# 768 unreachable matmuls and fifteen small loads in a gated decode kernel (attention beside a SwiGLU block)

## The chip, the core and the metric

The kernel runs on one core of one Trainium2 chip. Its time is the device time of one launch, in microseconds (us). The core has five engines, each with its own instruction stream: TensorE (PE in the profile; its weight loads are listed as PEld), VectorE (DVE), ScalarE (ACT), GpSimd (POOL) and SyncE (SP). Data is moved between the chip's memory (HBM) and the on-chip memory by 16 DMA engines, which take their work from queues. The engines wait for each other through semaphores; a DMA adds 16 to its semaphore in all, in steps as its shares land.

## The reference

One token `x` of 512 numbers goes through two blocks, and a gate mixes their results:

```python
def _A_ref(x, k_cache, v_cache, wq, wo):        # 32 query heads, 8 key/value heads, 32768 cached keys of 128
    q = (x @ wq) ...                            # by heads
    scores = einsum("bhqd,bhkd->bhqk", q, repeat(k_cache, 4)) * (128 ** -0.5)
    p = softmax(scores)
    o = einsum("bhqk,bhkd->bhqd", p, repeat(v_cache, 4))
    return o.reshape(1, 1, 4096) @ wo

def _B_ref(x, w_gate, w_up, w_down):            # 512 -> 1792 -> 512
    return (silu(x @ w_gate) * (x @ w_up)) @ w_down

g = sigmoid((x * gate_w).sum(-1))
return g * _A_ref(x, ...) + (1 - g) * _B_ref(x, ...)
```

All tensors are bf16. `k_cache` and `v_cache` are 64 MB each in powers of two (8 x 32768 x 128 x 2 bytes); they and the weights are read once, and the result is one row of 512 numbers.

## The kernel before

**Tiling.** The cache of one key/value head (a "group" of 4 query heads) is 8 MB of K and 8 MB of V. On chip the kernel keeps five pages of 32 KB a partition (`page`, line 177). Partition p holds the cached rows 256p to 256p + 255; each half of a group (128 rows a partition) fills one page. `load_k` and `load_v` are the functions on SyncE's queue that load a whole group of K or V, mostly with one DMA of 8 MB.

**Stages.** TensorE first computes q from `wq` and the two projections of the second block (`emit_start`). Then a loop of eight passes, one a group, does for K: transposes of 128x128 (`emit_fill`, line 371) into `pst`, copied to `ktT` by VectorE (line 765), then the scores (`emit_scores`, line 383) into `ps_sc`. The maximum is taken, ScalarE computes the exponentials into `ET`, and in the next pass TensorE multiplies them with V (`emit_v`, line 440) and reduces the sums (`emit_reduce`). When the loop is done, `emit_end` handles the last V, the product with `w_down` (`wd`, and a last part of it in `wz`), and begins the product with `wo`.

**The order on SyncE's queue.** It is written out by hand: `wq`, `w_gate`, `w_up`, K of group 0; then for g = 1 to 7 K of group g and V of group g - 1; then the last V, `wd` (line 350), two loads of the remaining 128 rows of `w_down` (line 358), and `wo` in five pieces (line 363). Most loads wait, on SyncE, until TensorE has done with the page that they overwrite: `load_k` on `sem_fill` (line 311), `load_v` on `sem_v_free` (line 335).

**TensorE's program.** It is written in another order than it runs. A loop of two turns holds two conditional parts: `emit_end`, for the second turn, stands first; `emit_start`, with the loop of eight passes in it, stands behind it and is taken in the first turn. Behind this whole block stands a tail that all engines have: TensorE adds the remaining pieces of `wo` (`emit_wo`, line 246, each piece behind a wait for its load), VectorE copies the sum into `res_row` (line 818), and SyncE and ScalarE each store half of it (line 270); SyncE then waits for both stores (line 822). Counted in the code, TensorE's program has 824 matmuls, each with a weight load of its own, and some 55 other instructions: about 1,700. Of these the loop of eight passes has about 1,080.

`emit_strip` is the helper that does one matmul of one column of weights against 512 columns. `PAD = 768` is already there: a tile `pad` of 768 bytes a partition, that nobody writes or reads.

## Time and profile before

| | |
|---|---|
| time, median of two runs | 349.05 us (348.97 to 349.12) |
| profiled execution: its time | 349.16 us |
| its span, first to last instruction | 347.8 us |
| bytes read from HBM | 148.11 MB, 426 GB/s over the span |
| busy: PE, PEld, DVE, ACT, POOL | 260.8, 220.6, 186.6, 33.4, 4.6 us |
| granted TensorE clock, mean | 0.851 |

The span is what the profile lists, from the first instruction of the program to the last; 1.4 us of the profiled execution's time lie around it. "Busy" is the time in which an engine worked; an engine's idle time is listed with what ended it. The chain of work is followed back from the last instruction, at each step to what released it, so its shares say what set the end. A DMA queue's share is the time that its packets took, out of the time of all 16 DMA engines. SPq stands for SyncE as an issuer of DMAs. "x" and a number is a count.

### The profile page before, as it was taken

To read this page: it belongs to the slowest core of one execution; us is meant where nothing else is said; L and a number is where in the kernel's file an instruction comes from. 1 tells how busy PE (TensorE), PEld (TensorE's weight loads), DVE (VectorE), ACT (ScalarE), POOL (GpSimd) and SP (SyncE) were. 2 spreads that over 40 slices of the span, in tenths; PEclk is the share of its full clock that TensorE was granted. 3 is DMA by queue.
4 is the path that set the end of the run, shared out by engine and by line. 5 is a ranking of instruction groups with operands and counts; after the bars stand their busy time and mean duration, and the time that the engine had idled before them with its cause. 6 is when DMAs were issued, how large, how long until landed. Compare 5 with 4: busy or idle time off the path is not lost.

```text
span 347.8 us, 8869 instructions
## 1 busy us (share of the span) xinstructions
PE 260.8 (75%) x3925; PEld 220.6 (63%) x3925; DVE 186.6 (54%) x232; ACT 33.4 (10%) x143; POOL 4.6 (1%) x16
## 2 busy tenths in 40 slices
PE   1354995999749982999459982999469972999475
PEld 1124994998449941997259942996269842996232
DVE  3144995698119931697129921895149820895101
ACT  1002000300130003000300003000400012000400
POOL 3000000000000000000000000000000000002000
PEclk9996999699659987699959985898869985898669
DMA  8999999999999999999999999999999999999996
GB/s 322 419 459 426 420 422 458 469 414 437 414 430 475 415 437 415 437 467 415 437 407 445 467 414 437 407 452 460 414 437 407 452 460 415 437 407 452 406 418 261
DMA packets 3946, 148.21 MB, mean 426 GB/s; under 512 B 450, under 2 KB 580, under 8 KB 868
## 3 DMA queue, kind: packets, MB, share of 16 engines
q1 hardware_dynamic: 3932, 148.11, 98.7%
q8 instruction: 6, 0.10, 0.1%
q10 hardware_dynamic: 8, 0.00, 0.0%
HBM read 148.11 MB, written 0.00 MB: 426 GB/s over the span
## 4 chain that ended last, share of the span: by engine, by line
DMA 64%; PE 33%; DVE 2%; issue 1%; SPq 1%; ACT 0%; DVEq 0%
DMA page<-in_A_k_cache_dram 52%; PE pst L371 24%; DMA page<-in_B_w_up_dram 6%; DMA page<-in_A_wo_dram 6%; PE ps_sc L383 5%; PE ps_o L440 2%; PE pst L535 1%; DVE ktT L722 1%; DVE ktT L765 0%; SPq L363 0%; PE ps_m L553 0%; PE ps_m L566 0%; DVE ktT L712 0%; DVE ktT L710 0%; PE ps_sc L246 0%
## 5 line engine op out<-in xcount | busy, mean ns | idle before, releaser
L765 DVE COPY ktT<-pst 128x2048 bf16<-128x2048 bf16 x128 | 153.3, 1221 | 64.6 <-PE pst L371 60.4
L371 PE MATMUL pst<-ident_f,page 128*128 128x128 f32 x1024 | 147.2, 299 | 39.5 <-DMA page<-in_A_k_cache_dram 38.2
L371 PEld LDWEIGHTS pst<-ident_f,page 128*128 128x128 f32 x1024 | 126.0, 154 | 43.9 <-DMA page<-in_A_k_cache_dram 38.8
L383 PE MATMUL ps_sc<-qcur,ktT 128*128 128x8 bf16 x2048 | 64.1, 166 | 6.3 <-DVE ktT L765 6.3
L383 PEld LDWEIGHTS ps_sc<-qcur,ktT 128*128 128x128 bf16 x2048 | 63.8, 97 | 8.0 <-DVE ktT L765 7.1
L440 PE MATMUL ps_o<-page,ET 128*16 128x512 bf16 x512 | 39.4, 477 | 5.5 <-DMA page<-in_A_v_cache_dram 5.5
L440 PEld LDWEIGHTS ps_o<-page,ET 128*16 128x16 bf16 x512 | 15.0, 107 | 26.1 <-issue 18.8
L633 ACT ACTIVATE ET<-ps_sc,nbias 128x128 bf16 x64 | 23.9, 555 | 49.9 <-DVE nbias L791 49.9
L626 ACT ACTIVATE acc<-ps_o 128x512 f32<-128x512 f32 x8 | 4.8, 597 | 223.8 <-PE ps_o L440 218.9
L783 DVE TENSOR_REDUCE gm<-ps_m 4x1 f32<-4x128 f32 x8 | 2.2, 279 | 40.6 <-PE ps_m L420 40.6
L633 ACT ACTIVATION_READ_ACCUMULATOR ET<-ps_sc,nbias 128x1 f32 x64 | 18.3, 285 | 0.0
L773 DVE TENSOR_REDUCE pmaxf<-ps_sc 128x4 f32<-128x512 f32 x16 | 11.0, 686 | 8.4 <-PE ps_sc L383 8.4
L497 PE MATMUL pst<-page,xT 128*1 128x512 bf16 x32 | 3.6, 627 | 8.9 <-DMA page<-in_A_wq_dram 8.9
L461 PE MATMUL ps_m<-sel,acc 128*128 128x4 f32 x64 | 8.4, 255 | 1.8 <-ACT acc L626 1.6
L461 PEld LDWEIGHTS ps_m<-sel,acc 128*128 128x128 f32 x64 | 7.7, 191 | 2.5 <-ACT acc L626 2.2
L424 PE MATMUL ps_m<-diag,ones_f 4*128 4x4 f32 x16 | 3.8, 306 | 6.8 <-DVE diag L787 6.8
L424 PEld LDWEIGHTS ps_m<-diag,ones_f 4*128 4x128 f32 x16 | 3.3, 259 | 8.4 <-issue 8.4
L750 DVE RECIPROCAL rS<-ps_m 128x4 f32<-128x4 f32 x9 | 1.6, 182 | 12.2 <-PE ps_m L461 12.2
L497 PEld LDWEIGHTS pst<-page,xT 128*1 128x1 bf16 x32 | 0.9, 115 | 10.7 <-issue 10.7
L685 DVE CAST ktT<-pst 128x1024 bf16<-128x1024 f32 x2 | 2.4, 1220 | 8.2 <-PE pst L497 8.2
L452 PEld LDWEIGHTS ps_m<-esum,ones_f 128*128 128x128 f32 x32 | 4.2, 190 | 3.5 <-issue 3.5
L301 POOL MEMSET page<- 48x2048 bf16 x1 | 1.8, 1798 | 311.7 <-PE pst L371 311.7
(76 smaller groups left out, 54.6 us busy)
## 6 DMA issues: line engine op xcount, KB each, us to landing
page<-in_A_k_cache_dram SPq DMA_DIRECT2D x4, 4096.0 KB, 34.9
page<-in_A_wq_dram SPq DMA_DIRECT2D x1, 4096.0 KB, 13.4
page<-in_A_wo_dram SPq DMA_DIRECT2D x1, 2048.0 KB, 17.4
page<-in_B_w_gate_dram SPq DMA_DIRECT2D x1, 1792.0 KB, 17.2
page<-in_B_w_up_dram SPq DMA_DIRECT2D x1, 1792.0 KB, 21.0
wd<-in_B_w_down_dram SPq DMA_DIRECT2D x1, 1664.0 KB, 30.3
page<-in_A_wo_dram SPq DMA_DIRECT2D x1, 1152.0 KB, 19.8
page<-in_A_wo_dram SPq DMA_DIRECT2D x1, 512.0 KB, 20.6
```

The source lines that it names most:

```text
L371: ins = pe.transpose(pst[u % NST][:, k * 128 : (k + 1) * 128], kv[:, n * 128 : (n + 1) * 128], ident_f[:, :],)
L383: ins = pe.matmul(ps_sc[b][:, col : col + 2 * HPG], kt[:, k, e, :], qcur[:, e, :], start=(e == 0), stop=(e == 1),)
L424: pe.matmul(ps_m[:, M_B0 : M_B0 + HPG], ones_f[0:HPG, :], diag[:, :], start=True, stop=True,).then_inc(sem_b, STEP)
L440: ins = pe.matmul(ps_o[32 * c : 32 * c + RQ * HPG, :], ET[:, n : n + RQ, :].rearrange("p n h -> p (n h)"), v[:, k * RQ : (k + 1) * RQ, :], ...
L452: pe.matmul(ps_m[:, M_S0 : M_S0 + HPG], ones_f[:, :], esum[:, b, :], start=(b == 0), stop=(b == NB - 1),)
L461: ins = pe.matmul(ps_m[:, M_P0 : M_P0 + HPG], acc[:, q, :], sel4[:, q * HPG : (q + 1) * HPG], start=(q == 0), stop=(q == RQ - 1),)
L497: ins = pe.matmul(pst[0][32 * k : 32 * k + 1, t * QN : (t + 1) * QN], xT[:, c : c + 1], wq_v[:, c, n : n + QN], start=(c == 0), stop=(c == ...
L535: ins = pe.matmul(pst[1][32 * k : 32 * k + 1, w * 512 : w * 512 + FS], xT[:, c : c + 1], wgu[:, w, c, k * FS : (k + 1) * FS], start=(c == ...
L626: act.activation(part, ps_o[:, :], ACT.Copy).then_inc(sem_acc, STEP)
L633: act.activation(ET[:, b * R : (b + 1) * R, h], sc[:, h, bass.ds(bank, R)], ACT.Exp, bias=nbias[:, h : h + 1], scale=SCALE, accum_out=esum ...
L765: dve.tensor_copy(ktT[:, n % NKT, :], pst[n % NST][:, :].bitcast(BF16)).then_inc(sem_cp, 1)
L773: dve.tensor_reduce(pmaxf[:, b, :], sc, AX.X, ALU.max).then_inc(sem_d, 1)
```

## The change

There are two additions; nothing is removed.

Behind the last matmul of TensorE's program stands a loop of two turns with two nested conditions, `turn > 0` and `turn < 1`. They exclude each other, so the 768 calls of `emit_strip` inside never run. TensorE runs the loop's own register instructions and branches, and skips the body.

On SyncE's queue there are fifteen new loads. The first takes 15 rows of 64 numbers (128 bytes each) from `A_wq` into the new tile `mark`, the next 14, and so on down to 1. One is issued behind each `load_k` and each `load_v` of the loop over the groups, and one behind the last `load_v`. Nobody reads `mark`. At the end SyncE waits for the fifteen loads, ahead of its wait for the stores.

```diff
+    MARKS = list(range(15, 0, -1))
+    PAD = 768
...
+        sem_mark = S_("s_mark")
...
         res_row = T("res_row", [128, 128], BF16)
+        mark = T("mark", [16, len(MARKS), 64], BF16)
...
+                marks = list(enumerate(MARKS))
+
+                def load_mark():
+                    if marks:
+                        m, n = marks.pop(0)
+                        sp.dma_start(mark[0:n, m, :], A_wq[0:n, 0:64]).then_inc(sem_mark, 16)
+
...
                 load_k(0)
                 for g in range(1, G):
                     load_k(g)
+                    load_mark()
                     load_v(g - 1)
+                    load_mark()
                 load_v(G - 1)
+                load_mark()
+                assert not marks
...
         for k in range(1, len(sem_wo)):
             ins = emit_wo(pe, k)
         ins.then_inc(sem_pe_sum, 1)
+        with pe.Fori(0, 2, 1) as turn:
+            with pe.If(turn > 0):
+                with pe.If(turn < 1):
+                    for _ in range(PAD):
+                        emit_strip(pe, wd, tT, 0, True, True)
         act.wait_ge(sem_pe_part, 1)
...
             emit_store(eng, half, res_row)
+        sp.wait_ge(sem_mark, 16 * len(MARKS))
         sp.wait_ge(sem_out, 32)
```

## The prediction

> **What bounds the kernel now.** I read the page's DMA part first, because the kernel reads everything once.

> ```profile
> q1 hardware_dynamic: 3932, 148.11, 98.7%
> q8 instruction: 6, 0.10, 0.1%
> q10 hardware_dynamic: 8, 0.00, 0.0%
> HBM read 148.11 MB, written 0.00 MB: 426 GB/s over the span
> ```

> SyncE's queue (q1) alone keeps the 16 DMA engines occupied for 98.7% of 347.8 us, or 343.3 us. Its first packet starts at 1.8 us and the last piece of `wo` lands at 345.9 us. So there is no hole in the stream: the time is the bytes over the rate, and what comes ahead and behind. The second row matters for this change: six packets of 16 KB (0.10 MB) that are instructions. The chain of waits, cut to its end, shows the tail:

> ```profile
> 324.78 20.75 DMA page<-in_A_wo_dram
> 345.53 0.04 issue
> 345.57 0.29 PE ps_sc L246 x8
> 345.87 0.04 issue
> 345.90 0.27 PE ps_sc L246 x4
> 346.17 0.02 issue
> 346.19 0.29 DVE res_row L818
> ```

> `wo` is issued at 323.5 to 325.3 us, is served 20 us later behind what was queued, and once it lands only 0.6 us of work and the store are left. The last of SyncE's instructions, the wait for the store, is at 347.82 us.

> When do the instruction packets run? The DMA view of 66 to 348 us answers:

> ```profile
> DMA packets 2881, 120.39 MB, mean 427 GB/s; under 512 B 336, under 2 KB 464, under 8 KB 752
> ...
> q1 hardware_dynamic: 2877, 120.39, 98.7%
> q10 hardware_dynamic: 4, 0.00, 0.0%
> ```

> There is no q8 row. The six packets start at 5.0, 36.8, 44.9, 51.3, 57.1 and 64.5 us. TensorE walks its loop of eight passes for the first time from 33 to 61 us; no other engine has a program that long. So I take them for TensorE's program, fetched block by block as it first gets there. Seven further passes, the jump back to `emit_end` and the tail fetch nothing: all of it stays on chip.

> **One fetch is felt by one DMA engine.** The steps in which a load's semaphore rises show its 16 shares. The first page of K, after one fetch, has 15 shares by 31.30 us and one at 32.29; V of group 0, after six, has ten shares from 79.02 to 79.66 and six from 80.58 to 80.98. So each fetch put another engine about 1.2 us behind, and it stays behind. The two small loads of the rest of `w_down` (line 358) then occupy four of the early ten for 0.61 us each time. At the end six shares of the last `wo` piece land from 344.13 to 344.33 and ten from 345.34 to 345.86: the slowest engine sets the end, and levelling all 16 would gain at most (345.86 - 344.2) x 6/16 = 0.6 us.

> **The change, part by part.**

> *The fifteen loads: bytes.* They move 15 + 14 + ... + 1 = 120 rows of 128 bytes, 15 KB. What counts is the engine that gets a share of each. A packet of 256 bytes took 15 ns, a semaphore packet 9 ns. For what lies between loads I compare the pieces of `wo` on the early engines: landings at 341.89, 343.15, 343.79, 344.13, so 1.26, 0.64 and 0.34 us for pieces of 4, 2 and 1 KB a row. Doubling the last gives 0.68 against 0.64: the fixed part of one load is at most 0.04 us. So a small load costs an engine between 0.02 and 0.06 us, and fifteen cost between 0 (an early engine gets them) and 0.9 us (the last engine gets all). I take 0.1 us, since most engines get fewer and the first ones to be served need not be the last.

> [...]

> *The fifteen loads: SyncE.* An issue costs SyncE 0.33 to 0.78 us (lines 311 and 358). It is hidden where SyncE waits anyway:

> ```profile
> SPq L311 <- PE pst L371: 130.6, 6, 28.7
> SPq L335 <- PE ps_o L440: 103.1, 6, 17.7
> ...
> SPq L335 <- PE pst L371: 22.8, 1, 22.8
> ...
> SPq L358 <- POOL page L301: 11.3, 1, 11.3
> ```

> Each of these waits is many times one issue. Two loads have no wait ahead of them and come later by one issue: V of group 0 (issued at 44.3, landed at 81.0) and `wd` (305.7, landed at 336.0). Both stand in the queue for 30 us and more, so the cost is nothing; without that cover it would be 0.4 to 0.8 us each. The added wait at the end stands ahead of the wait for the stores; the loads it asks for landed long before, so it costs one semaphore instruction, 0.02 us.

> *The 768 matmuls.* They add 1,536 instructions to some 1,700. None runs, but TensorE has to get past them. After the last wait for `wo` (345.90 us) it dispatches four matmuls and reaches the new loop at about 346.1. On the first turn it jumps over the whole body; the target lies 1,536 instructions on. Six packets or more hold the program of 1,700, so a block has under 290 instructions, and the target is some five blocks further, in one that was never fetched: the engine must wait for it. On the second turn the same target is on chip. VectorE's copy and the stores don't wait for this; the end of TensorE's program does.

> Nothing in the trace shows a jump to an absent block, so I bound it. From below: the store, on idle queues, is issued at 346.51 and its first data have landed at 347.61, 1.1 us; a 16 KB packet takes 0.61 us; 1.7 us together. From above: the second fetch of the trace cannot have been asked for before the loop began at 33.0, and its packet ended at 37.7 (36.83 + 0.88): 4.7 us, under a full load of data. The queues are idle at the end, so I stay nearer to the lower row and take 2.4 us. TensorE is through at 346.1 + 2.4 + 0.2 for the second turn = 348.7, against 347.82 for SyncE's last wait now: +0.9 us. At the lower end it is +0.2, at the upper one +3.2; and nothing if the end of TensorE's program is not what the time waits for.

> [...]

> *Sum.* 349.16 (profiled) + 0.1 + 0.0 + 0.9 = 350.2. The median before is 0.1 lower than the profiled execution, so I say 350.0 to the nearest half.

> **The rivals.**

> 1. *The jump hides.* The fetch is under 1.7 us, or the time does not wait for TensorE's end: 349.1 to 349.3. For it: 1.7 us pass between 346.1 and 347.8 anyway. Chance 0.25. Should the dead code not be in the program at all, the time is the same.
> 2. *The loop no longer stays on chip (slower).* If TensorE's fetches run ahead into the added blocks and push out blocks of the loop, the loop (1,080 instructions at under 290 a block) fetches about five blocks on each of seven passes. [...] For it: six blocks and what was there at the start are little over the program now, so there may be no more room. Against it: the dead code is never approached before the end, and the fetches of before went one block ahead only. Chance 0.10, nearly all of it above 356.
>    [...]
> 3. *Another engine is last.* The small loads, or other places for the fetched blocks, put the 1.2 us of a fetch and the 1.2 us of line 358's loads on one engine: +1.2 on top, 350.3 to 351.5. Chance 0.08.
> 4. *The small loads level the engines.* At most 0.6 us gained: 348.5. Chance 0.05; anything faster by more than that would need fewer bytes, 0.02.

> The forecast itself keeps 0.50. Within 2% (342.1 to 356.0, about what a measurement of this kernel can tell from no change) lie the forecast and rivals 1, 3 and 4: 0.88. Slower by over 2%: 0.10; faster: 0.02. The range must hold forecast, rival 1 and rival 3: from 348.8 to 353.0, which takes in the upper bound of the fetch (349.05 + 3.2 + 0.1 = 352.4).

> **What would show it.** In the profile of the changed kernel: fifteen more loads and no later landing of K and V than before; q8 with six packets until 66 us as before, and one or two more at 346 us or later; SyncE's last wait near 347.9; a gap on TensorE's sequencer behind the last matmul. q8 packets between 66 and 340 us would make rival 2 true and the prediction wrong; so would a hole in q1's stream behind a small load.

## The result, and the profile after

| | before | after |
|---|---|---|
| time, median (two runs each) | 349.05 us | 353.05 us (352.83 to 353.27) |
| ratio to before | | 1.0111, 95% interval 1.0094 to 1.0127 |
| profiled execution: time | 349.16 us | 352.83 us |
| its span | 347.84 us | 351.24 us |
| last share of `wo` landed | 345.86 us | 346.49 us |
| SyncE's last wait ended | 347.84 us | 348.54 us |

The change costs 4.0 us, or 1.1%. The forecast was 350.0 us, 0.95 us over before, in a range of 348.8 to 353.0: the direction and the main mechanism were right, the size was a quarter of what came, and the median lies 0.05 us above the upper end of the range.

The DMA part of the page of the changed kernel (queue, packets, MB, share of 16 engines):

```profile
q1 hardware_dynamic: 4172, 148.13, 97.9%
q8 instruction: 8, 0.13, 0.1%
q10 hardware_dynamic: 8, 0.00, 0.0%
HBM read 148.13 MB, written 0.00 MB: 422 GB/s over the span
```

q1 has 240 packets more, 120 of data and 120 of semaphores, and the instruction queue has two packets more. When these run is seen in the DMA view of two stretches of the changed kernel. From 66 to 346 us there is no instruction packet:

```profile
DMA packets 3076, 120.53 MB, mean 430 GB/s; under 512 B 534, under 2 KB 657, under 8 KB 945
...
q1 hardware_dynamic: 3076, 120.53, 99.6%
```

and from 346 to 352 us there are two, which the trace puts at 347.70 to 348.64 and 350.76 to 351.84 us:

```profile
q8 instruction: 2, 0.03, 2.1%
q1 hardware_dynamic: 13, 0.01, 0.3%
```

The end of the chain of waits, which follows the data and not TensorE's sequencer, is what it was, 0.69 us later:

```profile
325.57 20.92 DMA page<-in_A_wo_dram
346.49 0.04 issue
346.53 0.33 PE ps_sc L250 x4
346.86 0.02 issue
346.88 0.29 DVE res_row L838
```

SyncE still has time for its fifteen additional issues; its waits for pages, in the view of the DMA queue's own waits, are as long as before but for 5 us in all (130.6, 103.1 and 22.8 us before):

```profile
SPq L315 <- PE pst L386: 129.3, 6, 27.8
SPq L339 <- PE ps_o L455: 100.6, 6, 17.4
...
SPq L339 <- PE pst L386: 21.2, 1, 21.2
```

What comes last now is TensorE's sequencer, the part that runs the engine's register instructions and branches (PEldq in the rows). The views of the lines of the new loop (line 830 is the loop, lines 831 and 832 its outer and inner condition) give minimum, median and maximum in ns, then the first and the last start in us:

```profile
L831 PEldq COMPARE_BRANCH  x2: 77/1694/3310, 346.7 to 350.6; - x2
```

```profile
L832 PEldq COMPARE_BRANCH  x1: 217/217/217, 350.7 to 350.7; - x1
```

```profile
L830 PEldq MOVE  x3: 29/35/38, 346.5 to 350.5; - x3
L830 PEldq ALU_OP  x2: 36/36/36, 350.1 to 351.1; - x2
L830 PEldq COMPARE_BRANCH  x2: 76/158/240, 350.2 to 351.2; - x2
```

The branch of line 831 takes 3,310 ns on the first turn, where it jumps over the body, and 77 ns on the second, where it doesn't. On the second turn the inner condition jumps over the same body, and that takes 217 ns: what costs is the first jump to this place and not the distance. The first jump starts at 346.73 and ends at 350.04; the rest of the two turns ends with the span at 351.24, 2.70 us behind SyncE's last wait. In the span the 3.40 us are therefore 0.70 (everything up to the stores is later) and 2.70 (TensorE's sequencer behind them). Another 0.27 us lie outside the span (352.83 - 351.24 = 1.59 against 1.32). Its cause is open: 1.59 us lie outside in each of the three profiled executions that end with TensorE's program (this one and those with 768 and 192 matmuls below), though the second packet ends 0.6, 1.0 and 0.5 us behind the last instruction, and 1.3 to 1.4 us in all the others.

### The profile page after: what moved, and what is told of

The parts are those of the page before. It is cut to its first block, busy times and chain, and to the rows that moved or that the text cites. A ratio compares the mean times of both kernels' runs of the same rounds, so it can differ in the third digit from the quotient of the medians.

```text
span 351.2 us, 8894 instructions
## 1 busy us (share of the span) xinstructions
PE 260.5 (74%) x3925; PEld 220.3 (63%) x3925; DVE 186.7 (53%) x232; ACT 33.4 (10%) x143; POOL 4.6 (1%) x16
## 4 chain that ended last, share of the span: by engine, by line
DMA 63%; PE 32%; DVE 2%; issue 1%; SPq 1%; ACT 0%; DVEq 0%
DMA page<-in_A_k_cache_dram 51%; PE pst L386 23%; DMA page<-in_B_w_up_dram 6%; DMA page<-in_A_wo_dram 6%; PE ps_sc L398 5%; PE ps_o L455 2%; DVE ktT L780 1%; PE pst L550 1%; DVE ktT L737 1%; SPq L378 0%; PE ps_m L568 0%; PE ps_m L581 0%; DVE ktT L727 0%; DVE ktT L725 0%; ACT ktT L634 0%
```

## The experiments

Theory A: the jump goes to a block of the program that is not on chip, and TensorE's end comes last. Theory B: the small loads cost most. Theory C: a program twice as long disturbs the loop. All times of "before" below are medians of the runs made beside the experiment: 349.23 us for the body in `emit_start` and for the loads of one, twelve and sixteen rows, 349.15 us for the others.

### Only the unreachable matmuls

```diff
         ins.then_inc(sem_pe_sum, 1)
+        with pe.Fori(0, 2, 1) as turn:
+            with pe.If(turn > 0):
+                with pe.If(turn < 1):
+                    for _ in range(768):
+                        emit_strip(pe, wd, tT, 0, True, True)
```

> Only the 768 unreachable matmuls, without the fifteen loads. Theory A (the jump over the body goes to a block that is not on chip, and TensorE's end comes last): the branch takes about 3.3 us as in the changed kernel, its last instruction is 4.5 to 4.7 us behind the landing of the last piece of wo, and the time is +3.3 us (2.7 at least, 3.6 at most) over the kernel before. Theory B (the small loads cost most, by slowing the stream): under +1 us. Theory C (a program twice as long disturbs the loop): instruction packets between 66 and 340 us and a later landing of wo; A and B expect none and a landing as before, 345.9 us.

Measured: 352.45 us, ratio 1.0093 (1.0077 to 1.0108), +3.3 us. The last share of `wo` landed at 345.89 us, 0.03 later than before, and there is no instruction packet between 66 and 346 us. The branch over the body, in the view of its line:

```profile
L816 PEldq COMPARE_BRANCH  x2: 77/1874/3670, 346.1 to 350.3; - x2
```

Its 3.67 us can be split by the packet that it waits for: it starts at 346.13, the packet at 347.14 (1.0 us later), the packet takes 1.26 us, and the branch ends at 349.80, 1.4 us behind it. The other instructions of the two turns take 1.2 us more, to 351.02, which is 5.1 us behind the landing of `wo` and not 4.5 to 4.7. So theory A holds for 3.3 of the 4.0 us; B and C don't.

### Only the fifteen loads

```diff
+                def load_mark(): ...            # as in the changed kernel
...
+        sp.wait_ge(sem_mark, 16 * len(MARKS))
```

> Only the fifteen small loads, without the unreachable matmuls. Theory A: the time is what the stream loses, +0.5 to +0.7 us (the last piece of wo landed 0.63 us later in the changed kernel), and the span ends with SyncE's wait for the stores. Theory B: +3 to +4 us. If the 0.63 us was scatter between executions and not the loads: +0.0 to +0.2 us.

Measured: 349.73 us, ratio 1.0016 (1.0007 to 1.0025), +0.6 us. All 16 shares of the last `wo` piece came 0.59 us later on average, the last at 346.40 instead of 345.86. (The rows name no engine, so shares are compared in order of landing. In the four kernels of this section that leave out the loads and have the body behind or ahead of the tail, the mean differs from before by -0.08 to +0.01 us, single shares by up to 0.33.) With the run before this accounts for the whole change: 349.15 + 3.3 + 0.6 = 353.05.

### A shorter body: 128 and 192 matmuls

```diff
-                    for _ in range(768):
+                    for _ in range(128):        # and 192 in the other kernel
```

> 128 unreachable matmuls (256 instructions) and no small loads. [...] Theory A: the branch takes 0.1 to 0.3 us, no instruction packet behind 340 us, TensorE is through before the stores have landed, and the time is within 0.2 us of before. If the cost is that of the loop and its branches whatever they jump over: as much as with 768, +3.3 us. If it goes by the length of the body: a sixth, +0.5 us.

> [...] Theory A: a step, the branch takes 3.3 us again, one instruction packet behind 345 us or two, and the time is +2.7 to +3.6 us over the kernel before, as with 768. [...]

Measured: 349.22 us with 128 (ratio 1.0001, 0.9992 to 1.0010) and 352.56 us with 192 (ratio 1.0094, 1.0078 to 1.0109). The branch over the body with 128:

```profile
L816 PEldq COMPARE_BRANCH  x2: 77/202/328, 346.1 to 347.0; - x2
```

and with 192:

```profile
L816 PEldq COMPARE_BRANCH  x2: 77/1944/3810, 346.3 to 350.6; - x2
```

### The same body where the jump is hidden

The body stands in `emit_start`, ahead of the wait for `wq`.

```diff
                     pe.wait_ge(sem_dve_x, 1)
+                    with pe.Fori(0, 2, 1) as late:
+                        with pe.If(late > 0):
+                            with pe.If(late < 1):
+                                for _ in range(768):
+                                    emit_strip(pe, wd, tT, 0, True, True)
                     pe.wait_ge(sem_q, 16)
```

> The 768 unreachable matmuls stand in the first stage, ahead of TensorE's wait for wq, and no small loads. Theory A (what costs is a jump to an absent block at a place where the end waits for it): the jump falls at about 5 us, takes 3 to 4 us, and is hidden, since wq lands at 14.1 us; there are 7 to 9 instruction packets instead of 6, none behind 345 us unless the tail crosses into a new block; a second stall of up to 4 us may come at 316 us, where emit_end's block may have been replaced, and is hidden by loads that are queued until 336 us. Time -0.1 to +0.7 us. If the program's length itself costs (theory C): +3.3 us again, with instruction packets in every pass of the loop.

Measured: 350.55 us, ratio 1.0044 (1.0030 to 1.0058), +1.3 us: more than theory A said. The jump over the body and the jump from the loop back to `emit_end` both stall, in the view of their lines:

```profile
L493 PEldq COMPARE_BRANCH  x2: 77/2948/5818, 6.6 to 13.0; - x2
```

```profile
L609 PEldq COMPARE_BRANCH  x2: 67/3724/7381, 324.0 to 343.0; - x2
```

The first ends at 12.4 us, with `wq` landed at 14.3; the second ends at 331.4, with the last V landed at 333.4. Neither delays anything, though under a full load of data they take 5.8 and 7.4 us. In the kernel before the jump back to `emit_end` takes 209 ns (its line 604) and no instruction packet runs near it; here one starts at 329.1 us, and what it brings no row shows. What costs are the packets:

```profile
q1 hardware_dynamic: 3932, 148.11, 98.3%
q8 instruction: 11, 0.18, 0.2%
```

Eleven instead of six, where seven to nine were expected. The two early additional ones put two more shares of the stream 1.0 to 1.2 us behind. Three late ones start at 329.1, 334.6 and 343.2 us, and each puts a share that is late already another 1.2 us behind: one share of the last V (333.35), two of `wd` (337.29 and 337.43), three of the last `wo` piece (347.05 to 347.19). In the kernel before the last one lands at 345.86. So an instruction packet beside the stream is not free here: it puts shares about 1.2 us behind, and as these shares were late already, the last share of `wo` moved by 1.3 us.

### The same body ahead of the tail

```diff
+        with pe.Fori(0, 2, 1) as turn: ...      # the body of 768
         pe.wait_ge(sem_part, 1)
```

> The 768 unreachable matmuls stand ahead of the tail, between the first piece of wo and TensorE's wait for ScalarE's copy, and no small loads. Theory A: the same jump, with the same 3.3 to 3.8 us and 1.2 us for the rest of its two turns, but it begins at about 341.5 us, when TensorE would wait for the copy until 343.2 and for the last piece of wo until 345.9 anyway; the tail starts at 346.0 to 346.6 and needs 1.2 us, so the stores are 0.8 to 1.5 us late and nothing of TensorE's comes behind them: time +0.8 to +1.8 us, half of what it costs at the end. A cost that goes with the length of the program would be +3.3 us here too.

This expectation failed. Of six executions two took 352.93 and 353.42 us, 3.8 and 4.3 us more than before, and four took 360.0 to 360.1; none of the four was profiled, so what took 6.6 us more there stays open. In the profiled one (353.42) the jump starts at 343.1 and not at 341.5, because TensorE first goes through a drain and the barrier that ends the block (342.0 to 342.8), which I had not counted.

```profile
L811 PEldq COMPARE_BRANCH  x2: 77/1932/3787, 343.1 to 347.4; - x2
```

The end of the chain of waits of this kernel shows the other thing that I had wrong:

```profile
343.40 4.65 issue
348.05 2.38 PE ps_sc L246 x72
350.42 0.02 issue
350.45 0.29 DVE res_row L823
```

With nothing left to wait for, the tail's 72 matmuls take 2.4 us and not 1.2. They run at a granted clock of 0.50 here (348.0 to 350.5 us), where the kernel before had 1.00 for its tail (343.0 to 346.2): a weight load takes 150 ns instead of 97, a matmul 314 instead of 219. With a tail of 2.4 us the jump's 3.8 us are hidden only until 343.8, so that the tail still ends by 346.2, and here everything, stores included, is behind it.

### Small loads of one, twelve and sixteen rows

```diff
-    MARKS = list(range(15, 0, -1))
+    MARKS = [1] * 15                            # [12] * 15, [16] * 15
```

> Fifteen small loads of one row each at the places of the changed kernel, no unreachable matmuls. In the run with the loads alone all 16 shares of the stream came 0.58 us later, and nearly all of that grew between 98 and 195 us. Theory S (each share costs the DMA engine that serves it, 0.065 us): one share of the last wo piece +1.0 us, the other fifteen unmoved; the time +0.0 to +0.5 us. Theory L (each load holds up all engines alike, 0.04 us, whoever serves it): all 16 shares +0.6 us, time +0.6 us. Theory M (only loads of 9 to 13 rows cost anything, about 0.1 us on all engines): no share moves, time +0.0 us.

> Fifteen small loads of twelve rows each. Theory S: twelve shares of the last wo piece +1.0 us, four unmoved; time +0.5 to +1.0 us. Theory L: all 16 shares +0.6 us, time +0.6 us. Theory M: all 16 shares +1.5 us, time +1.5 us.

> Fifteen small loads of sixteen rows each, one row for each DMA engine. Theory S: all 16 shares of the last wo piece +1.0 us, time +1.0 us. Theory L: all 16 shares +0.6 us, time +0.6 us. Theory M: no share moves, time +0.0 us.

| rows in each of the fifteen loads | time | ratio, 95% | shares of the last `wo` piece, mean |
|---|---|---|---|
| 1 | 349.26 us | 1.0003 (0.9994 to 1.0012) | +0.07 us |
| 12 | 349.89 us | 1.0024 (1.0014 to 1.0033) | +0.58 us |
| 16 | 350.24 us | 1.0034 (1.0022 to 1.0046) | +0.63 us |
| 15 to 1 (the change) | 349.73 us | 1.0016 (1.0007 to 1.0025) | +0.59 us |

The last row was measured beside other runs of before, as said above. None of the three theories holds. With one row no share is 1.0 us late, against S, and the loads are nearly free, against L. With twelve rows the shares are not 1.5 us late and with sixteen not unmoved, against M. Sixteen rows cost S's 1.0 us of time, but only the last share came so much later; the mean is 0.63. What is left: the cost grows with the rows but less than they do, and it is spread: with twelve rows no share, in order of landing, moved by less than 0.27 us, though a load has only twelve to give.

### Small loads in a row, and twice as many

```diff
-                    load_mark()                 # behind each load_k and load_v
+                for _ in MARKS:                 # fifteen of twelve rows, behind the last load_v
+                    load_mark()
```

> Fifteen small loads of twelve rows, all one behind the other behind the last load of V (at 305 us), none between the earlier loads. With the same loads spread over the stream all 16 shares came 0.58 us later, and that grew only between 98 and 253 us. Theory N (each load costs the stream 0.04 us wherever it stands): shares of the last wo piece +0.5 to +0.7 us, time +0.6 us. Theory P (the cost hangs on the place in the stream): below 0.2 us, and then only on the engines that serve them.

Measured: 352.21 us, ratio 1.0084 (1.0071 to 1.0097), +3.1 us; the shares of the last `wo` piece came 2.15 us later on average and 1.07 to 3.24 us one by one. Five times the estimate: both theories fall. The view of SyncE's queue shows that the issues are no part of it, since `wd` is issued 19 us before it is served:

```profile
305.22 6.10 SPq L349 DMA_DIRECT2D mark<-in_A_wq_dram  x15
311.36 0.36 SPq L364 DMA_DIRECT2D wd<-in_B_w_down_dram  x1
```

The DMA view of 326 to 340 us of this kernel shows the stream itself thinned; in the kernel before the same stretch has 398 GB/s and 92.8%:

```profile
DMA packets 671, 4.71 MB, mean 337 GB/s; under 512 B 402, under 2 KB 402, under 8 KB 434
...
q1 hardware_dynamic: 671, 4.71, 85.9%
```

The steps of the semaphore that I take for those of the first engine to get there are at 330.44, .62, .79, .97, 331.14, .31, .49: 0.175 us a load, where the packets (13 ns of data and 9 ns of semaphore) make up 0.022. That is the price of one of these small loads where small loads stand one behind the other.

```diff
-    MARKS = [12] * 15                           # one at each place
+    MARKS = [12] * 30                           # two at each place
```

> Thirty small loads of twelve rows, two at each place of the changed kernel. Theory N: twice the 0.58 us, all shares +1.1 to +1.2 us, time +1.2 us. Theory P (each place costs once, or the loss has a ceiling): +0.5 to +0.7 us as with fifteen.

Measured: 350.92 us, ratio 1.0055 (1.0042 to 1.0068), +1.8 us; the shares came 1.09 us later on average, 0.18 to 1.7 one by one. The mean is nearly theory N's, twice the 0.58 us; the time is 0.6 us over it, since the latest share moved by 1.7. But N's rule, the same loss wherever a load stands, had failed in the run before.

With the loads spread out, the loss grows from about 80 to 200 or 250 us and hardly after (mean of the 16 shares in the changed kernel: 0.10 us at 80, 0.56 at 196, 0.59 at the end), though loads follow until 331 us. Rows are not the reason, since it is much the same with twelve in all.

The packets in the traces show where the loss sits. A data packet of 64 KB takes 2,418 ns, and in the kernel before 6 of 1,792 take more than 2,435. In the run with the loads alone 55 such packets lie between 98 and 178 us, most of them right behind a small load's packets, and take up to 2,678; from 196 us on there is none. With twelve rows there are such packets until 236 us. In the run with the loads alone all data packets of q1 together take 5.1 us longer than before and the small loads' own packets 2.6 us. Over 16 engines that is 0.49 us each, against 0.59 in the landings; the same sum gives 0.12 us with one row, 0.61 with twelve, 0.71 with sixteen and 0.98 with thirty loads, against 0.07, 0.58, 0.63 and 1.09. Why the packets behind a small load take longer in one part of the stream and not in another stays open.

None of these kernels is faster than the kernel before, and none points to one that would be.

## Why the prediction was right or wrong

- **What bounds the kernel.** Right: the stream's end and the tail decide, and q1 is dense in both kernels.
- **TensorE's program stays on chip; the dead code lies beyond what was fetched.** Right, and shown: no instruction packet between 66 and 346 us, and the step between 128 and 192 matmuls. Rival 2, which would have needed such packets, falls for this kernel. Rival 1 falls too: the time does wait for TensorE's end. So does rival 4: no share of the last `wo` piece, in order of landing, comes earlier than 0.43 us behind its old time.
- **The price of the jump.** This term was mis-sized: 2.4 us taken, 3.3 us measured in the changed kernel and 3.7 to 3.8 in three others. The bounds of 1.7 and 4.7 held. The lower row, a store's 1.1 us and 0.61 us for a packet, lacked the 1.4 us between the end of the packet and the end of the branch, and an instruction packet took 0.9 to 1.3 us at the end, not the 0.61 of a data packet; the prediction's own trace had 0.88 for one (36.83 to 37.7). The value was put nearer to that row than it should have been. Nor did the trace of before lack a jump that waits for a packet: in TensorE's first pass the branches of line 407 at 46.53 and 52.28 us took 754 and 1,303 ns and that of line 576 at 57.67 us took 1,817 ns, each until 1.4 us behind the end of an instruction packet (45.89, 52.19 and 58.07 us), where no branch of the two lines took over 210 ns in the later passes.
- **The second turn.** Also mis-sized: 0.2 us taken, 1.2 us measured. I counted a branch and there are seven instructions, with gaps of 0.06 to 0.15 us between them, two of them branches of 0.22 to 0.24 us.
- **The bytes of the small loads.** 0.1 us taken, 0.6 us measured, inside its bounds of 0 and 0.9. The step that failed is the one that takes a load's price from the packets and from three pieces of `wo`: 0.02 to 0.06 us; in a row of small loads each takes 0.175, and between large loads over half of the loss is that data packets, most of them right behind a small one, take longer, which a price read from the small packets can't have. The measured size lies inside the bounds, but not by this step. So the prediction's sign of no later landing of K and V did not come: they land up to 0.6 us later, and SyncE's last wait ends at 348.5 and not near 347.9.
- **SyncE's issues.** Right: 0.29 to 0.49 us each, the loads of V and `wd` later by one issue and no landing moved by it.
- **Rival 3**, an engine that gets one fetch too many: not in the changed kernel. The body in `emit_start` shows its like, two fetches on one engine: 1.3 us, near the 1.2 us that the prediction read from the landings.
- **The sum.** 0.1 + 0.9 was forecast; measured in the span are 0.7 + 2.7, and 0.27 outside it, which no step had and whose cause stays open.

## What to carry to other kernels

Code that never runs cost nothing measurable here with 128 matmuls, where the jump over it took 0.33 us (349.22 against 349.15 us); with 192 and 768, jumps that had to wait for an instruction packet took 3.3 to 3.8 us near the end of the stream and 5.8 and 7.4 under a full load of data, so see where the last jump of an engine lands, and keep it off the end. The time of this kernel is its DMA stream (98.7%), and packets beside it counted: an instruction packet put shares about 1.2 us behind, a load of twelve rows cost up to 0.175 us where its own packets take 0.022. Read the spread of the 16 shares of a late load's semaphore: before, the last piece of `wo` landed from 344.13 to 345.86 us, and TensorE went on with it only at 345.90.

## What the runs showed that I had not expected

- With 128 matmuls the branch takes 328 ns at most, and still one instruction packet starts, at 347.10 us, 1.0 us behind the start of the branch; nobody waits for it. In the kernel before, which doesn't jump there, no packet runs at the end. What the packet brings no row shows.
- The loads of 15 to 1 rows show which engines the instruction packets held up. In the changed kernel all shares of the loads of one to five rows land with the early shares of the stream; a load of six rows has one share with the late ones, one of seven to eleven has two, one of twelve three, one of thirteen four, one of fourteen five. So each shorter load seems to use the same engines as the longer one less the last, and of the six engines that served the instruction packets five are, counted by rows, the 6th, 7th, 12th, 13th and 14th, and the sixth is one of the last two. In the run with the loads alone the same count gives the 6th, 7th and 10th to 13th, so the places are not the same in every kernel. No row gives an engine's number; these places are read from the landings alone.
